# The first pair of expert blocks from counts taken before attention's last group

## The chip, the cores and the metric

The kernel runs on one core of a Trainium2 chip. Its metric is the device time of one execution in microseconds (us); the median of several executions is given, and one more execution was recorded by the hardware profiler. The names of the engines in what follows are those of the profile: PE is TensorE's matmul, PEld its weight load (which overlaps PE), DVE is VectorE, ACT is ScalarE, POOL is GpSimd, SP is SyncE, which here only issues DMAs. Each engine works through its own instructions in order; DMAs are issued from the queues of SP, ACT and POOL.

## The reference: what is computed

Three layers in a row, with B = 4, 8 heads, 768 positions, head width 48, so 3,072 tokens of width 384:

```python
for t in range(S):                        # attention, a delta rule per (batch, head)
    y[:, :, t] = einsum('bhd,bhde->bhe', q[:, :, t], state)
    v_old = einsum('bhde,bhd->bhe', state, k_n[:, :, t])
    state = state + bt * einsum('bhd,bhe->bhde', k_n[:, :, t], v[:, :, t] - v_old)
...
h = x @ w_in                              # first layer: 384 -> 2048 -> 384
x = np.maximum(0.01 * h, h) @ w_out
...
do_compute = x @ w_skip > 0               # expert layer, top 1 of 8
e_idx = argmax(x @ w_gate)                # gate_w is its softmax probability
y = gate_w * (np.maximum(x @ w1[e], 0) @ w2[e])     # w1: 384 x 1024, w2: 1024 x 384
out = x + y                               # for tokens with do_compute, else x
```

## The kernel before

**Stages.** Attention works in twelve groups of 256 tokens (a chunk of 128 positions of two batches). The first layer (`moe1`) takes each group of 256 rows when its attention is done: eight slices s of 256 hidden columns, `m_up` (matmuls into `ph`, L796) and, two slices later, `m_down` (L818 to L820, into `o`). All matmuls are split into high and low halves in fp16, so each product is three matmuls. Between them ACT copies `gg` out of PSUM (L801), DVE makes the leaky ReLU (L802), ACT casts the high half `ghh` (L804), and POOL makes the low half `gll` (L806). The twelfth group is done by `moe1_last`: it brings the ten columns with the scores first, so that the last route can start early.

**Route.** After each group `route` finds each token's expert and its place in that expert's part of the list `lst`, and POOL scatters the token numbers there, two scatters per group (L782); the second waits for the first. `store` writes the group's rows to `x2s` and to `out`, from SP's queue (from POOL's for the last group). "Route 10" is that of the eleventh group; the last route is route 11.

**Expert blocks.** A `Block` is 256, 128 ("small") or 64 ("tiny") rows of one expert. Its `tokens` loads its piece of the list (`ix`, L1189), gathers the rows from `x2s` (`xg`, L1192, one gather per 128 rows), and PE transposes them (L1200, into `pt`), from which ACT and DVE make `xh` and `xl`. Then come four `up` (L1215) and four `down` (L1233 to L1235), and `fin` scatters the result to `out` (L1246). Both the list loads and the gathers stand in POOL's queue. A gather reads `x2s`, so it waits for every store to it that was issued ahead of it. Weights of an expert are eight `ws` tiles of 384 KB, loaded from SP's queue (L1165, L1168), five in flight, and split by ACT (high, L460) and DVE (low, L461). Two successive "early" blocks belong to the same expert and share one set of weights.

**Tables.** Which expert and which rows a block has is known only at run time. `counts` takes the number of tokens per expert after a route (a matmul, L1041); `early` makes from it, after route 10, a table of up to six full blocks (pairs, from experts with at least 512 tokens so far); `tables` makes the other kinds' after the last route. SP and POOL read entries of a table with value loads (L1155). The order of blocks is fixed: four early, tiny, small, two early, then big ones (up to 256 rows, from what is left) with tiny and small ones between.

**Order.** `emit` interleaves the threads (attention's groups, `moe1`, `weights`, `tokens`, `moe2`) by a clock of PE's work; so it decides on each engine what stands ahead of what. `weights` holds the second expert's split until the last tables are placed (L1277).

Of the kernel before, what the change touches and what calls it, by code (L numbers as in the profile page):

```python
# [11 lines left out]
ALU = mybir.AluOpType  # L12
# [12 lines left out]
NE, F2 = 8, 1024  # L25
# [5 lines left out]
LR = 3072  # L31
BIG = 1 << 20
LOOK = 2
NEB, NSB, NSS, NTS = 6, 3, 3, 3
NBB = 20
NL = NE * LR + (NBB + 1) * 256
LOOK2 = 2
NET = 3, 3
NV = 8


# [471 lines left out]
def tile_kernel(ctx, tc, kq, ktok, vtok, bet, w_in, w_out, w_skip, w_gate, w1, w2, out):  # L513
    nc = tc.nc
    pool = lambda c, name, bufs, **k: c.enter_context(tc.tile_pool(name=name, bufs=bufs, **k))
# [213 lines left out]
    acc_state, routed, placed = [None], [-1], []  # L729
# [228 lines left out]
    n = len(groups)  # L958
# [14 lines left out]
    threads = [t for l in (tb, tv) for x in l for t in x.ts] + tz + tq + ta + tl + tn + tp + [Thread(loader()), tm]  # L973
# [11 lines left out]
    late = dict(side="right", reuse_waits="tile")  # L985
# [6 lines left out]
    e2 = pool(ctx, "e2", 2, **late)  # L992
    et = [pool(ctx, "et", 1, **late)]
    e3 = pool(ctx, "e3", LOOK2 + 2, **late)
    lctx = ctx.enter_context(ExitStack())
    m8 = pool(lctx, "m8", NS1 - LOOK - 2, **late)

    def moe1_last():
        i = n - 1
        scores = lambda s: m_down(i, s, slice(HD, XW), "r", ops2)  # L1000
        for s in range(NS1):
            yield from m_up(i, s, m8 if s < NS1 - LOOK - 2 else m3, h2)
            if s >= LOOK:
                yield from scores(s - LOOK)
        yield from m_down(i, 0, slice(0, HD), i)
        for s in range(NS1 - LOOK, NS1):
            yield from scores(s)
        sc = rp.tile([128, 2, 10], F32, tag="sc", name="sc")
        for t in range(2):
            nc.scalar.activation(out=sc[:, t], in_=ms["r"][t][:, HD:XW], func=AF.Copy, scale=2.0 ** -14)  # L1010
        threads.insert(0, Thread(high(last_route(i, sc), 150), lambda: "early" in state))
        for s in range(1, NS1):
            yield from m_down(i, s, slice(0, HD), i)
        xs = m_out(i, i, slice(0, HD))
        nc.vector.tensor_copy(out=xs[:, :, HD:HD + 1], in_=sc[:, :, 0:1])
        store(xs, first(i), nc.gpsimd)
        lctx.close()
        et.append(pool(ctx, "eu", 1, **late))

    def last_route(i, sc):  # L1020
        yield 0, 2
# [4 lines left out]
    t1 = lambda nm, shape, dt=F32: tbp.tile([1] + shape, dt, tag=nm, name=nm)  # L1026
# [7 lines left out]
    tt = lambda o, a, b, op: nc.vector.tensor_tensor(out=o, in0=a, in1=b, op=op)  # L1034
# [4 lines left out]
    def counts(nm):  # L1039
        pr = hps.tile([128, 512], F32, tag="h", name="cnt")  # L1040
        nc.tensor.matmul(pr[:, 0:NE], lhsT=ones16, rhs=acc_state[0], start=True, stop=True)  # L1041
        cnt = t1("cnt" + nm, [NE])
        nc.vector.tensor_copy(out=cnt, in_=pr[0:1, 0:NE])
        return cnt

    def above(x, first, nm, step=256.0):

        thr, gt, nb = t1("thr", [12]), t1("o", [NE, 12]), t1("nb" + nm, [NE])
        nc.vector.tensor_scalar(out=thr, in0=kio[:, 0:12], scalar1=step, scalar2=float(first), op0=ALU.mult, op1=ALU.add)
        tt(gt, col(x, 12), row(thr, NE), ALU.is_gt)  # L1050
        nc.vector.tensor_reduce(out=nb, in_=gt, axis=AX.X, op=ALU.add)
        return nb

    def upto(nb, nm):

        m, cb = t1("f", [NE, NE]), t1("cb" + nm, [NE])
        tt(m, tri8, row(nb, NE), ALU.mult)
        nc.vector.tensor_reduce(out=cb, in_=m, axis=AX.X, op=ALU.add)
        return cb

    def table(nb, cb, at, n, nm, step=True):
# [21 lines left out]
        state[nm] = tb  # L1083
        return last.ins

    def early():

        nb = above(counts("e"), 511.5, "e", 512.0)
        nc.vector.tensor_scalar(out=nb, in0=nb, scalar1=2.0, scalar2=None, op0=ALU.mult)
        cb = upto(nb, "e")  # L1090
        a, b, zero, taken = (t1(x, [NE]) for x in ("mine", "mina", "zero", "taken"))
        nc.vector.memset(zero, 0.0)
        table(nb, cb, zero, NEB, "early")
        tt(a, cb, nb, ALU.subtract)
        nc.vector.tensor_scalar_min(out=a, in0=a, scalar1=float(NEB))
        nc.vector.tensor_scalar_min(out=b, in0=cb, scalar1=float(NEB))
        tt(taken, b, a, ALU.subtract)
        state["taken"] = taken
        yield 0, 12
        for b in blocks[:3]:  # L1100
            yield from b.tokens()

    def tables():

# [28 lines left out]
    state = {}  # L1133

    class Block:


        def __init__(self, kind, k, ops):
            self.kind, self.k, self.ops = kind, k, ops

            self.of = blocks[-1] if kind == "early" and k % 2 else self
            self.loaded = self.split_ = 0
            self.ws, self.g = [None] * 8, {}
            self.tok = False
            self.nt = 1 if kind in ("small", "tiny") else 2
            self.rows = 64 if kind == "tiny" else 128
            self.slot = sum(b.nt == self.nt for b in blocks) % NET[self.nt - 1]
            blocks.append(self)
# [97 lines left out]
                nc.gpsimd.indirect_dma_start(out=out[:, :], out_offset=bass.IndirectOffsetOnAxis(ap=ix[:, t:t + 1], axis=0),  # L1246
                                             in_=y, in_offset=None, bounds_check=NT - 1, oob_is_err=False)

    order = [("early", 0), ("early", 1), ("early", 2), ("early", 3), ("tiny", 0), ("small", 0), ("early", 4), ("early", 5)]
    for k in range(NSB):  # L1250
        order += [("big", k)] + [(x, k + 1) for x in ("tiny", "small") if k < NSB - 1]
    blocks = []
# [4 lines left out]
    def weights():  # L1257
        own = [b for b in blocks if b.of is b]

        def more():  # L1260
            while sum(x.loaded - x.split_ for x in own) < 5:
                nxt = next((x for x in own if x.loaded < 8), None)
                if nxt is None or nxt.kind not in state:
                    break
                nxt.load()

        more()
        yield 0, 8
        for i, b in enumerate(own):
            if i > 2:  # L1270

                last = max(j for j, x in enumerate(blocks) if x.of is own[i - 3])
                yield 0, 0, lambda: ended[0] > last
            for _ in range(8):
                if b.loaded == b.split_:
                    yield 0, 0, lambda: more() or b.loaded > b.split_
                if i == 1 and not placed:  # L1277
                    yield 0, 0, lambda: placed
                with tc.issue_after(placed[0]) if i else nullcontext():
                    b.split()  # L1280
                more()
                yield 0, 0.7

    def tokens():
        for i, b in enumerate(blocks):
            if i < 3:
                continue
            same = [j for j in range(i) if blocks[j].nt == b.nt]
            yield 0, 0, lambda: b.kind in state and sum(j >= ended[0] for j in same) < NET[b.nt - 1]
            yield from b.tokens()  # L1290
# [22 lines left out]
        while pend:  # L1313
            yield from down()

    threads = [t for t in threads if not t.done] + [Thread(weights())]
    emit(threads, lambda: tm.done and routed[0] == n - 2)
    te = Thread(early())
    tl1 = Thread(moe1_last())
    threads = [te] + threads + [tl1]  # L1320
# [64 lines left out]
```

## Time and profile before

| | before |
|---|---|
| median of 3 runs | 1105.67 us (1105.28 to 1114.81) |
| the profiled execution | 1103.89 us |
| its span, first to last instruction | 1102.3 us |
| mean granted TensorE clock | 0.932 of 2.4 GHz |
| PE busy | 880.9 us, 80% of the span |
| PEld, DVE, ACT, POOL busy | 673.8, 699.7, 635.7, 517.7 us |
| DMA moved | 133.01 MB |

The profile's times are us from the start of the span. A row of the timeline gives the start, the duration, the engine, the line of the kernel, the operation with its output and inputs, the shape, how many such instructions in a row, and in brackets the time in which the engine was idle just before, with what ended that. Matmuls are pipelined, so the durations of neighbours overlap; the distance of their starts is what one costs.

### The profile page before, as it was taken

The numbers are of one execution on the slowest core, as the hardware profiler recorded it, in microseconds if no ns is written. First come the engines' busy times: TensorE is split into PE (matmuls) and PEld (weight loads), VectorE is DVE, ScalarE is ACT, GpSimd is POOL, SyncE is SP. The second block draws the span as 40 slices with busy tenths as digits, with TensorE's granted clock in tenths as the row PEclk, the third lists the DMA queues.
The fourth block names the chain that finished last, engine by engine and source line by source line (L and its number), as shares of the span: only waits on it lengthen the run. The fifth ranks groups of instructions, "written<-read, shape, count | busy, mean of one in ns | idle before, by whom it ended". The sixth has DMA issues, their size and how long they took to land. (4 is left out here: it accounts for less than half of the span.)

```text
span 1102.3 us, 26057 instructions
## 1 busy us (share of the span) xinstructions
PE 880.9 (80%) x10212; PEld 673.8 (61%) x10212; DVE 699.7 (63%) x1444; ACT 635.7 (58%) x1458; POOL 517.7 (47%) x536
## 2 busy tenths in 40 slices
PE   2167987578888778879878889899987689999893
PEld 1155765456666666657666567677765467676672
DVE  6889988758746878756657266332226575757850
ACT  4486587566867876748576657463333344545630
POOL 3567566473457566637464445352233252432110
PEclk9999987789999898989989899999999879999997
DMA  8844876662434455453412322200005376766820
GB/s 208 226 117 116 234 231 160 102 139 42 152 62 98 139 133 150 127 86 106 99 53 48 31 60 30 70 20 16 30 23 141 96 251 199 240 204 213 282 84 13
DMA packets 164880, 133.01 MB, mean 121 GB/s; under 512 B 87870, under 2 KB 146964, under 8 KB 164746
## 3 DMA queue, kind: packets, MB, share of 16 engines
q1 hardware_dynamic: 151696, 111.42, 38.4%
q10 hardware_dynamic: 8570, 10.76, 3.6%
q0 software_dynamic: 4480, 9.07, 2.7%
q8 instruction: 82, 1.34, 0.6%
q14 instruction: 52, 0.43, 0.2%
HBM read 101.68 MB, written 30.13 MB: 120 GB/s over the span
## 5 line engine op out<-in xcount | busy, mean ns | idle before, releaser
L806 POOL TENSOR_TENSOR gll<-gg,ghh 128x512 f16<-128x512 f32 x96 | 116.9, 1220 | 131.6 <-ACT ghh L804 117.0
L820 PE MATMUL o<-woh,gll 128*128 128x394 f16 (+2 forms) x416 | 128.1, 335 | 19.5 <-POOL gll L806 19.4
L796 PEld LDWEIGHTS <-wih 128*128 128x128 f16 x1152 | 115.7, 103 | 45.5 <-issue 22.5
L819 PE MATMUL o<-wol,ghh 128*128 128x394 f16 (+2 forms) x416 | 136.8, 334 | 0.0
L818 PE MATMUL o<-woh,ghh 128*128 128x394 f16 (+2 forms) x416 | 134.5, 333 | 1.0 <-ACT woh L640 0.9
L802 DVE SCALAR_TENSOR_TENSOR gg<-gg 128x512 f32<-128x512 f32 x96 | 78.5, 819 | 84.0 <-ACT gg L801 80.6
L263 POOL TENSOR_TENSOR gl<-g,gh 128x512 f16<-128x512 f32 x88 | 109.7, 1250 | 38.0 <-ACT gh L262 34.2
L254 ACT ACTIVATE g<-g,d 128x128 f32<-128x128 f32 x384 | 112.2, 389 | 18.6 <-PE g L251 10.5
L796 PE MATMUL ph<-xh,wih 128*128 128x256 f16 x576 | 103.5, 289 | 17.6 <-ACT gg L801 9.4
L796 PE MATMUL ph<-xl,wih 128*128 128x256 f16 x576 | 103.2, 287 | 1.1 <-DVE xl L726 1.1
L796 PE MATMUL ph<-xh,wil 128*128 128x256 f16 x576 | 102.6, 285 | 0.0
L255 POOL TENSOR_SCALAR_AFFINE_SELECT g<-g 128x512 f32<-128x512 f32 x96 | 71.1, 743 | 66.6 <-ACT g L254 65.9
L801 ACT COPY gg<-ph 128x512 f32<-128x512 f32 x96 | 57.4, 599 | 64.3 <-PE ph L796 60.8
L804 ACT CAST ghh<-gg 128x512 f16<-128x512 f32 x96 | 60.4, 630 | 46.8 <-DVE gg L802 46.5
L262 ACT CAST gh<-g 128x512 f16<-128x512 f32 x88 | 55.6, 636 | 41.1 <-POOL g L255 40.0
L1246 POOL DMA_INDIRECT out_dram<-y,ix x24 | 28.9, 1204 | 101.7 <-DVE y L1244 88.6
L782 POOL DMA_INDIRECT lst<-ids_i,pi x24 | 28.3, 1178 | 88.9 <-DMA lst<-ids_i,pi 53.3
L1215 PEld LDWEIGHTS <-w1h 128*128 128x128 f16 x720 | 58.5, 99 | 18.5 <-issue 8.8
L820 PEld LDWEIGHTS <-gll 128*128 128x128 f16 x416 | 40.1, 101 | 46.4 <-POOL gll L806 23.9
L1233 PE MATMUL o<-w2h,gh 128*128 128x384 f16 (+1 forms) x192 | 63.9, 333 | 1.0 <-ACT gh L1219 0.9
L796 PEld LDWEIGHTS <-wil 128*128 128x128 f16 x576 | 58.4, 103 | 10.1 <-issue 0.4
L1234 PE MATMUL o<-w2l,gh 128*128 128x384 f16 (+1 forms) x192 | 63.5, 331 | 0.0
(279 smaller groups left out, 2584.5 us busy)
## 6 DMA issues: line engine op xcount, KB each, us to landing
ws<-in_moe_w_dram SPq DMA_DIRECT2D x96, 384.0 KB, 5.2
kt<-in_ktok_dram SPq DMA_DIRECT2D x24, 384.0 KB, 3.9
x<-in_kq_dram SPq DMA_DIRECT2D x22, 384.0 KB, 4.3
sc<-hl SPq DMA_DIRECT2D x22, 384.0 KB, 3.0
raw<-in_moe_w_out_dram ACTq DMA_DIRECT2D x16, 384.0 KB, 4.7
ai<-gh SPq DMA_DIRECT2D x24, 256.0 KB, 2.8
vs<-in_vtok_dram SPq DMA_DIRECT2D x24, 192.0 KB, 3.5
x2s<-xs SPq DMA_DIRECT2D x22, 192.5 KB, 2.9
```

What stands on the lines that cost most here:

```text
L254: nc.scalar.activation(out=g32[:, j], in_=g[:, j], func=AF.Copy, scale=k["dd"][:, x, h:h + 1])
L255: nc.gpsimd.affine_select(out=g32, in_=g32, pattern=[[0, 4], [1, C]], compare_op=ALU.is_gt, fill=0.0, base=0, channel_multiplier=-1)
L263: nc.gpsimd.tensor_tensor(out=gl[:, hs], in0=g32, in1=gh[:, hs], op=ALU.subtract)
L796: nc.tensor.matmul(ph[:, j], lhsT=wt[:, d, fs], rhs=xx[:, d], start=(n == 0), stop=(n == 3 * KD - 1))
L802: nc.vector.scalar_tensor_tensor(out=g, in0=g, scalar=0.01, in1=g, op0=ALU.mult, op1=ALU.max)
L804: nc.scalar.copy(out=gh, in_=g)
L806: nc.gpsimd.tensor_tensor(out=gl, in0=g, in1=gh, op=ALU.subtract)
L818: nc.tensor.matmul(o, lhsT=gh[:, j, ts], rhs=wo[0][:, f, cols], start=(f == 0), stop=False)
L819: nc.tensor.matmul(o, lhsT=gh[:, j, ts], rhs=wo[1][:, f, cols], start=False, stop=False)
L820: nc.tensor.matmul(o, lhsT=gl[:, j, ts], rhs=wo[0][:, f, cols], start=False, stop=(f == NF1 - 1))
L1233: nc.tensor.matmul(o, lhsT=gh[:, j, ts], rhs=wh[:, f], start=(f == 0), stop=False)
L1234: nc.tensor.matmul(o, lhsT=gh[:, j, ts], rhs=wl[:, f], start=False, stop=False)
```

## The change

A new kind of block, "first", takes the first two places of the order (`NFB` = 2); the early ones go from six to four. A new thread, `beforehand`, starts as soon as `routed[0]` is n − 4, which is to say when only the routes of the last three groups are outstanding. It takes the counts of that moment, makes the table of the "first" pair by the rules that `early` had (now in `pairs`), lists and gathers both blocks' rows at once, and transposes them as the other threads leave room. `weights` starts loading with that table, among the last groups of the first layer. `early` then makes its table from the counts after route 10, less the blocks already taken. The second expert's split no longer waits for the last tables, only the third's does. The pool `eu` opens earlier, and the one-tile kinds ("tiny", "small") have two sets of buffers in place of three. With the reference's inputs the order of blocks still begins with two of one expert and two of another.

```diff
-NEB, NSB, NSS, NTS = 6, 3, 3, 3
+NFB, NEB, NSB, NSS, NTS = 2, 4, 3, 3, 3
...
-NET = 3, 3
+NET = 2, 3
...
+    et.append(pool(ctx, "eu", 1, **late))
...
-        et.append(pool(ctx, "eu", 1, **late))
...
+    def pairs(nm, had, n):
+
+        nb = above(counts(nm), 511.5, nm, 512.0)
+        at, a, b, taken = (t1(x + nm, [NE]) for x in ("at", "mine", "mina", "taken"))
+        nc.vector.tensor_scalar(out=at, in0=had, scalar1=256.0, scalar2=None, op0=ALU.mult)
+        stt(nb, nb, 2.0, had, ALU.mult, ALU.subtract)
+        cb = upto(nb, nm)
+        table(nb, cb, at, n, nm)
+        tt(a, cb, nb, ALU.subtract)
+        nc.vector.tensor_scalar_min(out=a, in0=a, scalar1=float(n))
+        nc.vector.tensor_scalar_min(out=b, in0=cb, scalar1=float(n))
+        tt(taken, b, a, ALU.subtract)
+        tt(taken, taken, had, ALU.add)
+        state["taken"] = taken
+
+    def beforehand():
+
+        zero = t1("zero", [NE])
+        nc.vector.memset(zero, 0.0)
+        pairs("first", zero, NFB)
+        gens = [b.tokens() for b in blocks[:NFB]]
+        for g in gens:
+            next(g)
+        yield 0, 12
+        for g in gens:
+            yield from g
+
     def early():
...
+        pairs("early", state["taken"], NEB)
+        g = blocks[NFB].tokens()
+        next(g)
         yield 0, 12
-        for b in blocks[:3]:
-            yield from b.tokens()
+        yield from g
...
-            self.of = blocks[-1] if kind == "early" and k % 2 else self
+            self.of = blocks[-1] if kind in ("first", "early") and k % 2 else self
...
-    order = [("early", 0), ("early", 1), ("early", 2), ("early", 3), ("tiny", 0), ("small", 0), ("early", 4), ("early", 5)]
+    order = [("first", 0), ("first", 1), ("early", 0), ("early", 1), ("tiny", 0), ("small", 0), ("early", 2), ("early", 3)]
...
-                if i == 1 and not placed:
+                if i == 2 and not placed:
                     yield 0, 0, lambda: placed
-                with tc.issue_after(placed[0]) if i else nullcontext():
+                with tc.issue_after(placed[0]) if i > 1 else nullcontext():
                     b.split()
...
     def tokens():
         for i, b in enumerate(blocks):
-            if i < 3:
+            if i <= NFB:
                 continue
...
-    threads = [t for t in threads if not t.done] + [Thread(weights())]
+    threads = [t for t in threads if not t.done] + [Thread(weights()), Thread(beforehand(), lambda: routed[0] >= n - 4)]
```

The rows below are the instructions as each engine has them in its program, first those of before, then those of the changed kernel. The first place is POOL's, around the two list scatters of route 10 (`lst<-ids_i,pi`; those of route 9 stand some rows ahead). Before, block 0's list (`ix<-lst`) comes behind both:

```order
L782 DMA lst<-ids_i,pi 29952x1
L806 TENSOR_TENSOR gll<-gg,ghh 128x512
L782 DMA lst<-ids_i,pi 29952x1
L806 TENSOR_TENSOR gll<-gg,ghh 128x512 x2
L1155 TENSOR_LOAD tbearly
L1155 ISA x2
L1189 REGISTER_ALU
L1189 DMA ix<-lst 128x2
L1155 TENSOR_LOAD tbearly
L1155 ISA x2
L806 TENSOR_TENSOR gll<-gg,ghh 128x512
```

In the changed kernel the piece begins with block 1's list load (block 0's stands just ahead of it) and ends with block 2's:

```order
L1207 DMA ix<-lst 128x2
L806 TENSOR_TENSOR gll<-gg,ghh 128x512
L1210 DMA xg<-x2s,ix 128x385 x4
L782 DMA lst<-ids_i,pi 29952x1
L806 TENSOR_TENSOR gll<-gg,ghh 128x512 x2
L782 DMA lst<-ids_i,pi 29952x1
L806 TENSOR_TENSOR gll<-gg,ghh 128x512 x2
L1173 TENSOR_LOAD tbearly
L1173 ISA x2
L1207 REGISTER_ALU
L1207 DMA ix<-lst 128x2
```

The four gathers of the first pair, and all that they wait for, stand ahead of route 10's scatters and of the last four `gll` of the first layer. SP's queue has, in the changed kernel, these rows where the weights start; before, the two `x2s` stores (of the eleventh group) stood right behind the two `out_dram` ones, and the value load and all `ws` behind them:

```order
L735 DMA out_dram<-xs 128x384 x2
L1173 TENSOR_LOAD tbfirst
L1173 ISA x2
L1183 ISA
L1183 DMA ws<-in_moe_w_dram 128x3x256
L1183 ISA
L1183 DMA ws<-in_moe_w_dram 128x3x256
L1183 ISA
L1183 DMA ws<-in_moe_w_dram 128x3x256
L733 DMA x2s<-xs 128x385 x2
```

Three loads of weights have moved ahead of the two stores for which the gathers wait. The second place is ACT's, from the `gg` copy of the last group's fourth slice on. Before, all eight copies are done ahead of the first weight split:

```order
L801 COPY gg<-ph 128x512
L804 CAST ghh<-gg 128x512
L801 COPY gg<-ph 128x512
L804 CAST ghh<-gg 128x512
L460 ACTIVATE w1h<-ws 128x3x256 x4
L1010 ACTIVATE sc<-o 128x10 x2
```

In the changed kernel the eight splits of the first expert's weights (`w1h`, `w2h`) stand among the copies of the fifth to the eighth slice:

```order
L801 COPY gg<-ph 128x512
L804 CAST ghh<-gg 128x512
L460 ACTIVATE w1h<-ws 128x3x256
L801 COPY gg<-ph 128x512
L460 ACTIVATE w1h<-ws 128x3x256 x2
L804 CAST ghh<-gg 128x512
L801 COPY gg<-ph 128x512
L460 ACTIVATE w1h<-ws 128x3x256
L460 ACTIVATE w2h<-ws 128x768
L804 CAST ghh<-gg 128x512
L460 ACTIVATE w2h<-ws 128x768 x3
L801 COPY gg<-ph 128x512 x2
```

The copy of the fifth slice is now behind one split, those of the last two behind all eight. The third place is PE's. Block 0's and block 1's transposes stand, but for the last, among the last group's `m_down` in the changed kernel. Between block 0's second up and its first down there are these rows, in which `pt<-ident,xg` is block 2's first three transposes:

```order
L1233 MATMUL ph<-xh,w1l 128x256
L1041 LDWEIGHTS ones_166
L1041 MATMUL cnt<-acc,ones_166 128x8
L1218 MATMUL pt<-ident,xg 128x128 x3
L1251 LDWEIGHTS gh
L1251 MATMUL o<-w2h,gh 128x384
L1252 LDWEIGHTS gh
```

So PE can't go on with block 0's first down until it has block 2's first rows. Before, the transposes that stood there were none; block 1's came within block 0's fourth up:

```order
L1215 MATMUL ph<-xh,w1l 128x256
L1215 LDWEIGHTS w1h
L1215 MATMUL ph<-xh,w1h 128x256
L1200 MATMUL pt<-ident,xg 128x128 x3
L1215 LDWEIGHTS w1h
```

## Rows read from the trace of the kernel before

**Rows 1.** Busy time by stretch: length, PE, PEld, DVE, ACT, POOL, clock, DMA share, GB/s
```profile
838.00:863.00 25.00, 18.78 (x121) 10.58 (x119) 11.67 (x37) 13.41 (x21) 4.88 (x5) 0.86 0.79 220
863.00:905.00 42.00, 30.43 (x195) 21.82 (x195) 26.26 (x82) 11.87 (x18) 18.09 (x19) 0.80 0.48 150
905.00:1085.00 180.00, 171.84 (x1529) 125.33 (x1526) 115.50 (x171) 89.01 (x148) 48.74 (x46) 1.00 0.61 195
```
**Rows 2.** PE's waits from 836 to 905: total us, times, longest
```profile
PE pt L1200 <- DMA xg<-x2s,ix: 14.3, 3, 8.5
```
**Rows 3.** PE's timeline, from 815 to 905
```profile
817.95 0.49 PE L796 MATMUL ph<-xh,wih 128*128 128x256 f16 x3
...
854.80 0.55 PE L1200 MATMUL pt<-ident,xg 128*128 128x128 f32 x3 [2.77 <-DMA xg<-x2s,ix]
...
863.01 0.82 PE L1215 MATMUL ph<-xh,w1h 128*128 128x256 f16 x6 [1.36 <-ACT xh L1202]
...
866.94 0.33 PE L1233 MATMUL o<-w2h,gh 128*128 128x384 f16 x1
867.10 0.33 PE L1234 MATMUL o<-w2l,gh 128*128 128x384 f16 x1
...
881.30 0.90 PE L1200 MATMUL pt<-ident,xg 128*128 128x128 f32 x3 [8.54 <-DMA xg<-x2s,ix]
...
897.84 0.88 PE L1200 MATMUL pt<-ident,xg 128*128 128x128 f32 x3 [3.02 <-DMA xg<-x2s,ix]
```
**Rows 4.** PE by stretch: length, busy, granted clock, DMA share, GB/s
```profile
856.00:859.40 3.40, 3.40 (x17) 0.50 0.98 321
881.30:886.70 5.40, 5.40 (x21) 0.50 0.28 100
897.80:903.80 6.00, 5.96 (x26) 0.50 1.04 322
```
**Rows 5.** POOL's timeline, from 825 to 905
```profile
829.25 0.99 POOL L782 DMA_INDIRECT lst<-ids_i,pi  x1 [1.19 <-PE cnt L1041]
...
834.46 0.99 POOL L782 DMA_INDIRECT lst<-ids_i,pi  x1 [3.03 <-DMA lst<-ids_i,pi]
835.48 2.27 POOL L806 TENSOR_TENSOR gll<-gg,ghh 128x512 f16<-128x512 f32 x2
842.37 0.61 POOL L1189 DMA_DIRECT2D ix<-lst  x1 [4.62 <-DMA lst<-ids_i,pi]
...
849.49 1.10 POOL L1192 DMA_INDIRECT xg<-x2s,ix  x1 [5.27 <-DMA ix<-lst]
850.90 1.00 POOL L1192 DMA_INDIRECT xg<-x2s,ix  x1 [0.31 <-issue]
...
875.20 1.73 POOL L1189 DMA_DIRECT2D ix<-lst  x3 [7.26 <-DMA lst<-ids_i,pi]
...
887.45 4.18 POOL L1192 DMA_INDIRECT xg<-x2s,ix  x1 [3.25 <-DVE w1l L461]
```
**Rows 6.** DVE's timeline: the early table's first and last row, one long row, weight splits
```profile
829.11 0.15 DVE L1043 COPY cnte<-cnt 1x8 f32<-1x8 f32 x1
...
834.99 2.79 DVE L1065 TENSOR_SCALAR of<-kio 1x8 f32<-1x8 f32 x1
...
837.96 0.16 DVE L1082 TENSOR_SCALAR tbearly<-sm 1x6 int32<-1x6 f32 x1
...
886.26 3.55 DVE L461 SCALAR_TENSOR_TENSOR w1l<-ws,w1h 128x768 f16<-128x768 f32 x4
```
**Rows 7.** SP's timeline: the first issues of weights
```profile
835.96 2.23 SPq L1165 DMA_DIRECT2D ws<-in_moe_w_dram  x4
```
**Rows 8.** ACT's timeline: the first and the last split of block 0's weights
```profile
845.56 0.84 ACT L460 ACTIVATE w1h<-ws 128x768 f16<-128x768 f32 x1 [6.20 <-DMA ws<-in_moe_w_dram]
...
854.26 0.84 ACT L460 ACTIVATE w2h<-ws 128x768 f16<-128x768 f32 x1 [0.16 <-DMA ws<-in_moe_w_dram]
```
**Rows 9.** The page's DMA issues: count, KB each, median us from issue to landing
```profile
ws<-in_moe_w_dram SPq DMA_DIRECT2D x96, 384.0 KB, 5.2
```

More of the change, by code (lines that the diff above doesn't have):

```diff
@@ L1084, in table @@
         return last.ins
-    def early():
[L1088 to L1098, printed above, removed]
+    def pairs(nm, had, n):
[21 more added lines that the diff above has]
+            yield from g
+    def early():
+        pairs("early", state["taken"], NEB)
+        g = blocks[NFB].tokens()
+        next(g)
         yield 0, 12
-        for b in blocks[:3]:
-            yield from b.tokens()
+        yield from g
     def tables():
```

## The prediction

> **What bounds the kernel now.** I read the busy table first, then the work by stretches, then PE's waits there, then the engines that it waits for. From 905 us on PE is busy 171.84 of 180.00 us at full clock [rows 1], so the end moves with whatever PE loses ahead of 905. Two stretches are thin: 838 to 863, 18.78 us of 25.00 busy, and 863 to 905, 30.43 of 42.00 [rows 1]. In both, PE waits for gathered rows: 14.3 us in three waits [rows 2]. The rows of PE's timeline show them at 854.80 (2.77), 881.30 (8.54) and 897.84 (3.02), with a 1.36 wait for ScalarE's cast at 863.01, where block 0's first matmul starts [rows 3]. After the three gaps the granted clock stands at 0.50 to 0.51, which is the lower of its two levels: 3.4 us from 856.0, 5.4 us from 881.3, 6.0 us from 897.8 [rows 4]. Half of such a stretch is lost.
>
> So from block 0's first matmul (863.01) on, PE loses 8.54 + 3.02 of waiting and (5.4 + 6.0)/2 = 5.7 of clock: **17.3 us**. That is all that earlier blocks can win there. Ahead of 863.01 it also loses 2.77 + 1.36 and 1.7 of clock to the same cause.
>
> Why the rows are late is read from POOL [rows 5]. The first `lst` scatter of route 10 goes at 829.25, the second at 834.46, because it waits 3.03 for the first. The list load of block 0 goes at 842.37, the gathers at 849.49 and 850.90, and PE has the rows at 854.80: 25.5 us from the first scatter. Block 1's list load stands at 875.20, behind the last route's scatters (7.26 idle for them).
>
> **What the change moves, and the costs.** Nothing is computed twice: the counts of the reference's inputs give one expert 1,111 tokens after ten groups, so both "first" blocks are full, and the number of blocks stays. PE gets one counting matmul, DVE 39 operations on one partition, and the one-tile blocks (tiny and small) keep two of their three slots. The lost slot I cost at nothing: what covers it is the block of 256 rows that stands between two pairs of one-tile blocks in the order, about as long as the 12.4 us that a list load and its gather take (842.37 to 854.80 [rows 5, 3]); were that cover gone, each of three such blocks could wait a part of 12.4.
>
> *Table.* The count goes where PE stands at 817.95 [rows 3]. In the kernel before, the early table takes DVE from 829.11 to 838.12 [rows 6], 9.0 us; the first table has a few rows more. One of its rows takes 2.79 instead of 0.15, beside two `gll` of POOL at 835.48 that take 2.27 [rows 5, 6]; the same `gll` stand beside the new table, so I repeat 9.0: ready at 827.2 (2 us earlier if no row is held), and SP's first `ws` at 827.7.
>
> *Rows.* On SP group 10's `x2s` stores now stand behind three `ws`. Four issues took 2.23 [rows 7], so the stores go at 829.6. What they then take is not shown: the first `ws` of before came 9.6 us after its issue (835.96 to ScalarE's split at 845.56 [rows 7, 8]), all `ws` on the median 5.2 [rows 9]. I take the 9.6, since they go into the queue right behind those first loads: 839.2, 840 for the second; the gathers start at 840.6. The lower end is 835.1, set by the list load (842.37 until its gather at 849.49 is 7.1, from about 828).
>
> *POOL.* Four gathers at 1.4 each (849.49 to 850.90) hold POOL until 846.2. Behind them in order: the first scatter of route 10, two `gll`, the second scatter 5.2 later, two `gll`. These scatters went at 829.25 and 834.46 before, so they lose 17 us. That is the price of the change: the last group's four `gll` end at 846.2 + 5.2 + 1.0 + 2.3 = 854.7. Behind the last of them PE has, by the order, 59 matmuls, 50 of them at 0.163 (the rows 866.94 and 867.10 [rows 3]) and the rest tiny: 8.4. **Block 0 starts at 863.1**, as before, although it waits for nothing of its own any more. ScalarE could spoil this: by the order its copy of the last group's fifth `gg` stands behind the first weight split, and the last two copies behind all eight, since ScalarE works in order. The eight take 9.5 us (845.56 to 855.10 [rows 8]). From 827.7 + 9.6 = 837.3, with the copies between them, that is 848, and the last `gll` could go at 851; POOL comes to it at about 853.5. So PE's last ups wait some 6 us for their buffer, but under the wait for `gll`; the cover is 2 us thick, and what goes beyond it shifts block 0. Route 10 also starts some 3 us later on DVE; its scatters wait for the gathers anyway.
>
> *Block 2.* Its list needs route 10's second scatter. I take the chain of before, 25.5 from the first scatter: 846.2 + 25.5 = 871.7. PE's order puts its first transposes behind block 0's first two ups. Two ups are 863.01 to 866.94, 3.93 [rows 3], with the transposes and the last route's few matmuls between them 4.6. PE gets there at 867.7 and waits 4.0. From 871.7 it goes on as if block 0 had started at 867.1. Against 863.0 that is a loss of 4.1, plus 1.7 of clock (3.4 us at half, as after the gap of 2.77). Block 3's rows need the last route's scatters and block 0's slot; they come in POOL's order before PE's place for them at about 895 to 900, at no cost, 2 us if late. The second expert's weights are issued behind the first's and used only after blocks 0 and 1, some 30 us of PE later.
>
> **Sum:** 17.3 − 4.1 − 1.7 = 11.5 us less than the profiled execution's own 1103.89: 1092.4. The median of the runs is 1105.67, 1.8 above that execution, so 1094.2; I say **1094**. About 1% (11 us) is what a measurement of this kernel can tell from no change: faster is below 1094.6, slower above 1116.7.
>
> One rule speaks against the change. The row: in one case a gather's issue took 4.18 on POOL, at 887.45, while DVE ran four weight splits without a break from 886.26 (3.55) [rows 5, 6]; those at 849.49 and 850.90 took 1.10 and 1.00, beside single splits. The Trainium skill, page "SBUF — State Buffer", section "🔬 SBUF: two separate sides", says that VectorE and GpSimd share a port pair as a lock held for a whole instruction, and that GpSimd cannot write its DMAs' descriptors while VectorE holds it. The 4.18 row and the 2.79 row agree with it, the 1.00 row doesn't ask for it. By that rule all six gathers that now stand beside splits would take 4.18, as priced under the third rival.
>
> **Rivals.**
> 1. *Fast start* (1088.5): the first loads don't lag, the gathers go at 835.1. Route 10's scatters, the `gll` and block 2's rows all come 5.5 earlier; block 0 starts at 857.6, the wait for block 2 stays 4.0. The gain is 11.5 + 5.5 = 17.0: 1086.9, or 1088.5 on the median. For it: the 5.2 of all `ws` [rows 9]. Against it: the 9.6 of the first [rows 7, 8].
> 2. *The wait moves* (1101): block 2's gather is as slow as that of 887.45, which PE waited for until 897.84, 10.4 instead of the 5.3 of 849.49 to 854.80 [rows 5, 3], some 6 us more with its longer issue, because block 1's weights load beside it. PE waits 10 instead of 4, and loses 1.3 more of clock: 1092.4 + 7.3 = 1099.7, 1101.5 on the median.
> 3. *Gathers held by splits* (1114): DVE now splits block 0's weights where the four gathers issue, and block 1's where block 2's two do. At 4.18 each instead of 1.02, six give 19.0 on POOL, all ahead of block 2's rows: 890.7. As if block 0 had started at 886.1, with 3 us of clock: 23.1 + 3.0 − 17.3 = 8.8 slower, 1112.7, 1114.5 on the median. It decides from four such gathers on (12.6 us, above the 11.5 gained); block 3's two would add 6.3 more. For it: the 4.18 row. Against it: the two gathers of 1.10 and 1.00, and that a split waits for a `ws` of its own, which breaks the run of splits.
> 4. *No effect* (1105.7): block 0 and 1 wait as before. The order speaks against it.
>
> **How the numbers follow.** Forecast 0.42 (1090 to 1098), fast start 0.25, moved wait 0.22, held gathers 0.08, none 0.03. Faster by over 1%: the fast start and about half of the forecast, 0.47. Slower by over 1%: the worse part of the third rival, 0.05. Within: 0.48. The range 1086 to 1107 holds the forecast, the moved wait, no effect and most of the fast start, 0.84.
>
> **What would show it.** Block 0's first up within 2 us of 863, with no wait for its transposes; no wait for block 1's rows at all; one wait of about 4 us for block 2's, right behind two ups; the first `lst` scatter of route 10 at about 846; ScalarE idle up to 837 for the first `ws`. The forecast is wrong if the gathers issue near 835 or after 843, if any of them takes 4 us, or if PE waits for something else ahead of 905: the counts' rows on DVE, or the first expert's weights. After 905 PE should be as busy as now.

## The result and the profile after

The changed kernel's median is 1082.41 us (1077.43 to 1092.28, 4 runs); the kernel before, 1105.47 with the run taken beside it (1097.59 to 1114.81, 4 runs). The comparison of the runs gives a ratio of 0.987, 95% interval 0.9827 to 0.9912: 1.3% faster, within 0.9 and 1.7%. On 1105.5 that is 1091, where 1094 was forecast. The ratio is not the quotient of the two medians: these lie further apart, by 23 us, and 1082.41 itself stands below the forecast's range of 1086 to 1107. The run named `again` below, beside many more of before on one chip, gives 1090.41 against 1102.46, ratio 0.9892 (0.9846 to 0.9938).

The profiled execution of after took 1081.11 us. How much of the distance to 1103.89 belongs to the change is read from one place that both programs have, the last one up to which PE's program is the same. In the changed kernel the first count stands there, at 808.93; the kernel before has no such count, and reaches the same place at 817.95 [rows 3]. So 9.0 us of the distance lie in front of the change. The twelve other profiles have that place between 810.0 and 822.4 us (the table below): the front differs from run to run. From this place ("the count" in what follows) to PE's last matmul it took 265.5 us before (to 1083.43) and 251.5 after (to 1060.47), 14.0 less. This stretch, "the changed part", is what the experiments compare.

Where in it: PE's waits after, from 815 to 905 (total us, times, longest), against the 14.3 us for gathers of [rows 2]:

```profile
PE pt L1218 <- DVE xl L1221: 4.9, 2, 2.7
PE o L820 <- POOL gll L806: 3.5, 2, 2.8
PE o L818 <- ACT ghh L804: 1.8, 1, 1.8
PE pt L1218 <- DMA xg<-x2s,ix: 1.1, 1, 1.1
```

The waits for gathered rows have gone but for 1.1 us. In their place PE waits twice for `xl`, DVE's low half of the rows just transposed, which must leave PSUM before the next transposes go in. PE's timeline after, around block 0's start (start, duration, idle before in brackets), answers to [rows 3]:

```profile
850.04 0.55 PE L1218 MATMUL pt<-ident,xg 128*128 128x128 f32 x3 [2.28 <-DVE xl L1221]
...
853.84 0.49 PE L1233 MATMUL ph<-xh,w1h 128*128 128x256 f16 x3
...
857.98 0.55 PE L1218 MATMUL pt<-ident,xg 128*128 128x128 f32 x3 [2.66 <-DVE xl L1221]
...
860.24 0.84 PE L1233 MATMUL ph<-xl,w1h 128*128 128x256 f16 x3
...
863.03 0.53 PE L1218 MATMUL pt<-ident,xg 128*128 128x128 f32 x3
863.40 0.33 PE L1251 MATMUL o<-w2h,gh 128*128 128x384 f16 x1
```

Block 0's first matmul stands 44.9 us after the count (853.84 − 808.93; before 45.1), its first down at 54.5 (before 866.94 − 817.95 = 49.0). A triple of `ph` takes 0.64 instead of 0.33 behind the second of the two waits: the granted clock is 0.50 to 0.53, about its lower level, from 859.0 to 862.5. Block 2's transposes at 863.03 wait for nothing. POOL's timeline after, the answer to [rows 5]:

```profile
828.05 1.09 POOL L1210 DMA_INDIRECT xg<-x2s,ix  x1 [6.44 <-DMA ws<-in_moe_w_dram]
829.44 1.04 POOL L1210 DMA_INDIRECT xg<-x2s,ix  x1 [0.30 <-issue]
830.79 1.01 POOL L1210 DMA_INDIRECT xg<-x2s,ix  x1 [0.30 <-issue]
832.10 1.75 POOL L1210 DMA_INDIRECT xg<-x2s,ix  x1 [0.30 <-issue]
834.15 1.11 POOL L782 DMA_INDIRECT lst<-ids_i,pi  x1 [0.30 <-issue]
...
839.76 1.00 POOL L782 DMA_INDIRECT lst<-ids_i,pi  x1 [2.20 <-DMA lst<-ids_i,pi]
...
847.78 0.60 POOL L1207 DMA_DIRECT2D ix<-lst  x1 [4.72 <-DMA lst<-ids_i,pi]
853.69 1.17 POOL L1210 DMA_INDIRECT xg<-x2s,ix  x1 [5.31 <-DMA ix<-lst]
```

The profile puts the 6.44 in front of the first gather down to a weight load, which a gather doesn't need; it reads `x2s`, and the two stores to it had landed by 827.06. The first pair's gathers go 19.1 us after the count, route 10's first scatter at 25.2, block 2's gathers at 44.8 and 46.2. And the work from block 0's first down to the end, before and then after (length, PE busy, granted clock, DMA share, GB/s):

```profile
866.00:1084.00 218.00, 199.28 (x1697) 0.96 0.59 190
```

```profile
863.40:1061.00 197.60, 190.77 (x1679) 1.00 0.61 196
```

That is the gain: the granted clock is 1.00 on the mean instead of 0.96, and PE's idle time falls from 18.7 us to 6.8.

### The profile page after: what moved, and what is told of

Same layout as the page of the kernel before. It is cut to its first block, busy times and chain, and to the rows that moved or that the text cites. A ratio compares the mean times of both kernels' runs of the same rounds, so it can differ in the third digit from the quotient of the medians.

```text
span 1079.5 us, 26091 instructions
## 1 busy us (share of the span) xinstructions
PE 872.8 (81%) x10213; PEld 670.1 (62%) x10213; DVE 707.7 (66%) x1474; ACT 634.6 (59%) x1458; POOL 512.3 (47%) x536
## 5 line engine op out<-in xcount | busy, mean ns | idle before, releaser
L796 PEld LDWEIGHTS <-wih 128*128 128x128 f16 x1152 | 113.5, 101 | 45.0 <-issue 24.0
L802 DVE SCALAR_TENSOR_TENSOR gg<-gg 128x512 f32<-128x512 f32 x96 | 80.8, 842 | 83.7 <-ACT gg L801 82.9
L796 PE MATMUL ph<-xh,wih 128*128 128x256 f16 x576 | 101.1, 283 | 19.7 <-ACT gg L801 11.9
L1264 POOL DMA_INDIRECT out_dram<-y,ix x24 | 25.2, 1052 | 97.5 <-DVE y L1262 85.5
L461 DVE SCALAR_TENSOR_TENSOR w1l<-ws,w1h 128x768 f16<-128x768 f32 x48 | 45.1, 955 | 32.5 <-ACT w1h L460 32.2
L782 POOL DMA_INDIRECT lst<-ids_i,pi x24 | 26.4, 1102 | 79.9 <-DMA lst<-ids_i,pi 54.6
```

Source lines behind the costliest of these rows:

```text
L796: nc.tensor.matmul(ph[:, j], lhsT=wt[:, d, fs], rhs=xx[:, d], start=(n == 0), stop=(n == 3 * KD - 1))
L802: nc.vector.scalar_tensor_tensor(out=g, in0=g, scalar=0.01, in1=g, op0=ALU.mult, op1=ALU.max)
```

## The experiments

All kernels of the table were compared with the kernel before on the same chip; the ratio is to it. The columns after it come from one profile each, in us: the place of the first count (`before` and `b_net` have none: for the one it is the place above, for the other it is worked out from the early count at 827.17, 10.92 behind it in the kernel before), and, counted from there, block 0's first up, its first down, and PE's last matmul (its start); then the time from that down to the last matmul.

| kernel | ratio (95%) | count at | first up | first down | last matmul | down to last |
|---|---|---|---|---|---|---|
| before | 1 | 817.95 | 45.1 | 49.0 | 265.5 | 216.5 |
| changed | 0.987 (0.9827, 0.9912) | 808.93 | 44.9 | 54.5 | 251.5 | 197.1 |
| again | 0.9892 (0.9846, 0.9938) | 814.85 | 48.3 | 54.6 | 258.2 | 203.6 |
| rows_late | 1.0117 (1.0035, 1.0199) | 815.04 | 51.4 | 56.4 | 274.9 | 218.5 |
| w_late | 0.9896 (0.9827, 0.9965) | 819.87 | 50.7 | 56.8 | 256.6 | 199.8 |
| one_early | 0.9941 (0.9905, 0.9976) | 810.03 | 46.4 | 52.5 | 253.9 | 201.4 |
| hold | 0.990 (0.987, 0.9931) | 819.90 | 42.6 | 50.1 | 247.8 | 197.7 |
| undo_hold | 0.9925 (0.9886, 0.9964) | 818.59 | 50.5 | 54.8 | 252.3 | 197.5 |
| x2s_first | 0.9883 (0.9807, 0.9959) | 817.69 | 43.0 | 53.8 | 250.2 | 196.5 |
| hold_x2s | 0.9877 (0.9819, 0.9936) | 821.32 | 44.3 | 55.9 | 255.9 | 200.0 |
| quiet | 0.9883 (0.9836, 0.993) | 820.73 | 41.1 | 53.6 | 255.9 | 202.3 |
| quiet_hold | 0.9879 (0.9828, 0.9929) | 822.36 | 45.7 | 51.8 | 253.2 | 201.5 |
| quiet_hold_x2s | 0.9899 (0.9852, 0.9947) | 815.52 | 48.6 | 53.1 | 255.7 | 202.6 |
| b_net | 0.9968 (0.9926, 1.0009) | 816.25 | 45.0 | 48.9 | 265.0 | 216.0 |

The last column splits the table in two: the eleven profiles in which POOL has block 1's list and gathers ahead of the last route's scatters have 196.5 to 203.6, the three in which it has them behind (`before`, `b_net`, `rows_late`) 216.0 to 218.5. The places of block 0 show no such split.

**again**: no edit.

> The changed kernel once more, beside the kernel before on the same chip. In the two profiles the first count matmul stands at 808.93 (before, the same place: 817.95) and PE's last matmul at 1060.47 (before: 1083.43). So the changed part takes 251.5 us where it took 265.5, 14.0 less; the other 9.0 us lie in attention and in the first layer, where both programs have the same PE rows. Theory: only the 14 us belong to the change; the ratio stays at 0.987 (1091 by the before of 1105.5) and the changed part at 250 to 253. Rival: the front is really faster (by the other placement of buffers): the ratio comes to 0.979 and the place of the first count lies 9 us ahead of that of the kernel before again.

The ratio came as the theory has it, the changed part longer than it said, 258.2: two profiles of one program are 6.6 us apart. They lie behind block 0's first down, where PE waits 6.0 us for gathered rows instead of 1.8, and where one stretch of 50 us (from 180 after the count) has PE busy for 44.04 instead of 46.61, at a granted clock of 0.93 instead of 1.00. So a single profile can't tell 4 us. The front was not ahead again (814.85, within the spread of the table).

**rows_late**: the rows after route 10 again, the weights early. `beforehand` makes only the table; POOL reads its entries from a copy that DVE makes behind the early table, and `early` fetches the rows of the first three blocks.

```diff
-        gens = [b.tokens() for b in blocks[:NFB]]
-        for g in gens:
-            next(g)
-        yield 0, 12
-        for g in gens:
-            yield from g
+        yield 0, 0
...
-        g = blocks[NFB].tokens()
-        next(g)
         yield 0, 12
-        yield from g
+        for b in blocks[:NFB + 1]:
+            yield from b.tokens()
```

> The changed kernel with the first pair's lists and rows fetched only after route 10 again, as before; its weights still come early. Theory (the rows are the gain): the waits for block 0's and block 1's gathers are back, the changed part takes 262 to 268 us, no faster than before. Rival (the weights' earlier loads are a good part of the gain): 255 to 259.

The whole gain is gone, and 1.2% more; the changed part, 274.9, is longer than the theory's 262 to 268. PE's waits of this kernel, and the rows on PE's timeline behind them:

```profile
PE pt L1219 <- DMA xg<-x2s,ix: 12.9, 2, 11.4
PE pt L1219 <- DVE xl L1222: 5.0, 2, 4.0
```

```profile
864.94 0.90 PE L1219 MATMUL pt<-ident,xg 128*128 128x128 f32 x3 [4.03 <-DVE xl L1222]
866.42 1.44 PE L1234 MATMUL ph<-xh,w1h 128*128 128x256 f16 x6 [0.58 <-ACT xh L1221]
883.67 0.87 PE L1219 MATMUL pt<-ident,xg 128*128 128x128 f32 x3 [11.41 <-DMA xg<-x2s,ix]
```

The long wait for block 1's rows is back, 11.4 instead of 8.54 [rows 3]. So late rows cost the gain. But these rows are later than those of before: block 0's list load goes 35.2 us after the count (850.28) instead of 24.4 (842.37 [rows 5]), and on DVE the low halves of the first expert's weights now stand among the rows of the early table, which is ready 33.6 us after the count instead of 20.2. So this kernel doesn't show what early weights are worth with rows no later than before; whether they are needed, the next one shows.

**w_late**: the rows early, the first expert's weights as late as before (SP reads the index from the same kind of copy).

```diff
-    threads = [t for t in threads if not t.done] + [Thread(weights()), Thread(beforehand(), lambda: routed[0] >= n - 4)]
+    threads = [t for t in threads if not t.done] + [Thread(weights(), lambda: "later" in state), Thread(beforehand(), lambda: routed[0] >= n - 4)]
```

> The changed kernel with the first pair's rows early as they are, but the first expert's weights loaded only after the early table is written (after route 10, as before). The count that begins the changed part stands 45 us ahead of block 0's first matmul. Theory (the rows are the gain, the weights only have to be there): the stores to x2s no longer stand behind three weight loads, so the four gathers go 3 to 4 us earlier; the weights land about 40 us after the count and hold block 0 by a few us; ratio to the kernel before 0.985 to 0.995, changed part 249 to 256. Rival (the weights beside the first layer's last groups are needed): block 0 and block 2 wait for weights, 260 or more.

The first load goes 18.5 us after the count, where the kernel before had 18.0. The gathers go at 834.72, 14.9 after the count, as the theory has it, and the ratio, 0.9896, is that of `again`; the changed part, 256.6, is just above the theory's range. Block 0 starts later (50.7), but not for its weights: PE waits 3.78 us until 870.23 for block 2's rows, whose transposes stand ahead of block 0's first up in this kernel. The weights need not be early: the rows alone bring the gain.

**one_early**: block 1's list and rows together with block 2's, after route 10: the first edit is in `beforehand`, the second in `early`.

```diff
-        gens = [b.tokens() for b in blocks[:NFB]]
+        g = blocks[0].tokens()
...
-        g = blocks[NFB].tokens()
+        gens = [b.tokens() for b in blocks[1:NFB + 1]]
```

> The changed kernel with block 0's rows early, but block 1's list and rows after route 10, with block 2's. Theory: route 10's scatters come earlier on POOL, since only two gathers or none stand ahead of them, and block 1's rows are there in time, because it starts some 16 us after block 0; what counted is that neither waits for the last route's scatters: 248 to 256 us, as the changed kernel. Rival (the early rows of block 1 are the gain, its 8.54 us wait and 2.7 of clock): 260 or more.

The changed part is 253.9, as the theory has it, and far from the rival's 260; the ratio, 0.9941, lies just above the upper ends of the changed kernel's two intervals (0.9912 and 0.9938). PE waits 6.1 us for gathers, in three waits of at most 3.1. So it is enough to lift block 1 over the last route's scatters; whether its still earlier place is worth the half per cent isn't settled, since the intervals overlap.

**hold** and **undo_hold**: when the second expert's splits run. In `hold` they are ordered behind block 1's last `xh` on ACT (`last.lh`) and its last `xl` on DVE (`last.ll`):

```diff
+                last = blocks[NFB - 1]
+                if i == 1 and not last.tok:
+                    yield 0, 0, lambda: last.tok
...
-                with tc.issue_after(placed[0]) if i > 1 else nullcontext():
-                    b.split()
+                with tc.issue_after(last.lh if i == 1 else placed[0]) if i else nullcontext():
+                    with tc.issue_after(last.ll) if i == 1 else nullcontext():
+                        b.split()
```

In `undo_hold` that part of the change is taken back:

```diff
-                if i == 2 and not placed:
+                if i == 1 and not placed:
...
-                with tc.issue_after(placed[0]) if i > 1 else nullcontext():
+                with tc.issue_after(placed[0]) if i else nullcontext():
```

> The changed kernel, with the second expert's splits ordered behind block 1's last xh on ACT and its last xl on DVE. In the changed kernel PE waits 2.28 and 2.66 for DVE's xl behind those splits, right around block 0's first ups, and the clock is at half for 3.5 us after. Theory (the splits that run too early cause this): both waits go, 5 to 6.6 us less in the changed part, 245 to 247 us. Rival (the splits are then late for block 2, whose ups come about 31 us after block 0's): PE waits for block 2's weights, the part takes 251 or more.

> The changed kernel with one part undone: the second expert's split waits for the last tables again. Theory: on DVE the low halves come after the last tables, some 20 us later, on ACT most high halves still stand ahead of xh; so one of the two waits of PE for xl stays: 248 to 251 us for the changed part. Rival (the low halves are needed earlier, the early split is a part of the gain): block 2 waits for its weights, 255 or more.

In `hold` the waits for `xl` are gone, and one of 2.7 has come, which the profile puts down to DVE's row `f` of the last tables:

```profile
PE o L818 <- ACT ghh L804: 2.8, 1, 2.8
PE pt L1218 <- DVE f L1034: 2.7, 1, 2.7
PE o L820 <- POOL gll L806: 2.3, 4, 0.7
```

On PE's timeline this wait stands behind the ups, ahead of block 2's first transposes:

```profile
866.08 0.49 PE L1233 MATMUL ph<-xl,w1h 128*128 128x256 f16 x3
869.32 0.52 PE L1218 MATMUL pt<-ident,xg 128*128 128x128 f32 x3 [2.75 <-DVE f L1034]
```

A transpose reads nothing of the tables. It reads block 2's rows, and their first gather, issued at 864.99, landed at 869.18. So this is read as the wait for block 2's rows that the prediction has; in `hold_x2s` below the same transposes wait 5.71 us, there put down to the gather itself. The first down comes 4.4 us earlier (50.1), and the part is the shortest of all, 247.8, between the theory's 245 to 247 and the rival's 251. In `undo_hold` neither wait for `xl` stays, against the theory; PE waits 4.8 for the last route's `oh` on DVE instead, and the part is 252.3, just above the forecast 248 to 251. Against the kernel before, 0.990 and 0.9925: the whole kernel doesn't show the 4 us.

**x2s_first** and **hold_x2s**: SP stores group 10's rows (the last of `stored`) ahead of the first loads of weights.

```diff
-                nxt.load()
+                with tc.issue_after(stored[2 * (n - 1) - 1]):
+                    nxt.load()
```

> The changed kernel with group 10's two stores to x2s ahead of the first weight loads on SP. In the changed kernel POOL is idle for 6.4 us until these stores have landed, 8 us after their issue, then issues the gathers at 828.05, 19.1 us after the count. Theory (the loads in front delay the stores): the gathers go 3 to 4 us earlier, at 15 to 16 us after the count, route 10's scatters and the last gll with them; PE's waits for gll and block 0's start come forward by 2 to 4 us; changed part 248 to 251. Rival (the gathers wait for something else, the list): no earlier than 19.

> The edits of hold and x2s_first together, with the first expert's splits among the last group's copies as in the changed kernel. Theory: the waits for xl go (hold: 4.5 us to block 0's first down), the gathers go earlier but one of them meets an unbroken run of splits on DVE again and takes over 4 us: 245 to 250 us, ratio 0.983 to 0.989. Rival: the fourth gather takes 1.0 to 1.8 as in the changed kernel.

The gathers of `x2s_first` go 14.9 after the count, where the changed kernel has 19.1: the loads in front did delay the stores. (Block 0's list doesn't explain the 19.1: in the changed kernel it had landed at 824.94, 2.1 us ahead of the second store.) POOL's timeline, and then DVE's beside the fourth gather:

```profile
832.61 1.08 POOL L1210 DMA_INDIRECT xg<-x2s,ix  x1 [2.25 <-DMA x2s<-xs]
...
835.33 1.00 POOL L1210 DMA_INDIRECT xg<-x2s,ix  x1 [0.30 <-issue]
836.64 4.59 POOL L1210 DMA_INDIRECT xg<-x2s,ix  x1 [0.31 <-issue]
841.53 1.04 POOL L782 DMA_INDIRECT lst<-ids_i,pi  x1 [0.30 <-DVE w2l L461]
```

```profile
837.36 0.94 DVE L461 SCALAR_TENSOR_TENSOR w1l<-ws,w1h 128x768 f16<-128x768 f32 x1
...
838.37 0.94 DVE L461 SCALAR_TENSOR_TENSOR w1l<-ws,w1h 128x768 f16<-128x768 f32 x1
...
839.42 0.94 DVE L461 SCALAR_TENSOR_TENSOR w1l<-ws,w1h 128x768 f16<-128x768 f32 x1
...
840.53 0.96 DVE L461 SCALAR_TENSOR_TENSOR w2l<-ws,w2h 128x768 f16<-128x768 f32 x1
```

The fourth gather takes 4.59 while DVE splits without a break, as the one of 887.45 in [rows 5, 6], and eats 3.6 of the 4.2 us won. In `hold_x2s` the same gather took 4.78, and block 2's first one 3.33 beside three splits, for whose rows PE then waited the 5.71. The part of `x2s_first`, 250.2, is in the expected range; that of `hold_x2s`, 255.9, is not (245 to 250). By the ratio neither kernel is told apart from the changed one.

**quiet**, **quiet_hold**, **quiet_hold_x2s**: the first expert's splits behind the last group's copies (`tail` holds ACT's and DVE's last rows of the last `m_up`), then with the other two edits.

```diff
+                if i == 0 and not tail:
+                    yield 0, 0, lambda: tail
...
+                with tc.issue_after(placed[0] if i else tail[0]) if i != 1 else nullcontext():
+                    with tc.issue_after(tail[1]) if i == 0 else nullcontext():
```

> The changed kernel with the first expert's splits ordered behind the last group's last gg and ghh on DVE and ACT; their loads still start early. In the changed kernel ACT's copy and cast of the last slices stand behind splits that wait for their loads, and PE waits 1.8 to 3.1 us for ghh; on DVE the splits run beside the four gathers, whose fourth took 1.75 and 1.83 us in two runs, and 4.59 where the splits ran without a break. Theory: PE's wait for ghh goes, all four gathers take about 1.0 us; block 0's splits then come later, and block 0 starts no earlier, since only five loads are ahead: changed part 246 to 252 us. Rival (the splits are then what block 0 waits for): 254 or more.

> The edit of quiet and that of hold together: the first expert's splits behind the last group's copies, the second's behind block 1's last xh and xl. Theory: PE's waits for ghh and for xl both go, 3 + 4.5 us and the clock around them; changed part 243 to 247, ratio to the kernel before 0.980 to 0.986. Rival (ACT and DVE then have 16 splits ahead of block 2 and the wait moves to block 0's gh or block 2's weights): 250 or more, ratio 0.988 to 0.995, no better than the changed kernel.

> As quiet_hold, and the stores to x2s ahead of the weight loads on SP. Theory: the four gathers go some 15 us after the count (19.1 in the changed kernel) at 1.0 us each, so route 10's scatters and block 2's rows come 4 to 5 us earlier; as nothing splits beside them, the gain of x2s_first is not lost to a gather of 4.59: 241 to 246 us, ratio 0.978 to 0.985, the fastest. Rival: no wait for rows is left to be won, so it equals quiet_hold.

With no split beside them all four gathers are quick, in `quiet` and here in `quiet_hold_x2s`, from 14.9 after the count on:

```profile
830.45 1.17 POOL L1212 DMA_INDIRECT xg<-x2s,ix  x1 [2.27 <-DMA x2s<-xs]
831.92 1.01 POOL L1212 DMA_INDIRECT xg<-x2s,ix  x1 [0.30 <-issue]
833.24 1.00 POOL L1212 DMA_INDIRECT xg<-x2s,ix  x1 [0.30 <-DVE tbearly L1084]
834.54 0.99 POOL L1212 DMA_INDIRECT xg<-x2s,ix  x1 [0.30 <-issue]
```

But PE then waits elsewhere, in `quiet_hold_x2s`:

```profile
PE o L822 <- POOL gll L806: 6.7, 1, 6.7
PE pt L1220 <- DMA xg<-x2s,ix: 2.9, 1, 2.9
PE o L1253 <- ACT gh L1239: 2.9, 1, 2.9
```

PE waits 6.7 for the last `gll` of POOL, which stands there behind block 2's list load (849.18, idle for 5.80 before it, for route 10's second scatter), then for ACT, which now has the late splits ahead of block 0's `gh`. In `quiet` PE waits 4.0 for block 0's own rows and 4.0 for `xl`, behind splits that had waited for their loads; in `quiet_hold` 4.0 for block 0's rows and 3.7 for `oh`. The expected 0.980 to 0.986 and 0.978 to 0.985 did not come: 0.9879 and 0.9899, and 0.9883 for `quiet`, whose part is 255.9, which is its rival's value. The parts of the other two, 253.2 and 255.7, missed their ranges as well. In these kernels shortening one of the waits ahead of block 0's downs gave the next one, and none can be told from the changed kernel.

**b_net**: `NET = 2, 3` alone, in the kernel before.

> The kernel before with one edit of the change alone: two sets of buffers for the tiny and small blocks in place of three. Theory (the lost slot is covered by the blocks of 256 rows between): 1.000, within 0.4%. Rival (the slots are awaited): up to 12 us more, 1.005 to 1.011.

0.9968, the interval holds 1; the changed part and block 0's places are those of the kernel before. There the third slot was not awaited.

## Why the prediction was right, step by step

- **The 17.3 us that go.** From block 0's first down on, the profile of before has 216.5 us, the changed kernel 197.1 and 203.6 in two profiles, 19.4 and 12.9 less: 16.2 on the mean. `w_late` (199.8, the rows early and the weights not) and `rows_late` (218.5, the weights early and the rows not) show that it is the rows. Right, as closely as two profiles that differ by 6.5 can tell.
- **Block 0 starts where it did.** Forecast 45.1 after the count, measured 44.9 and 48.3. The 44.9 is in part luck. POOL's last `gll` ended at 843.05, 34.1 after the count instead of 36.8, and a wait for `xl` that the forecast did not have (2.28 at 850.04) took most of these 2.6 us back. Without this wait block 0 would have started at 42.6, as it does in `hold`. The terms on the way were off too: the table took 7.9 instead of 9.0 (DVE 809.17 to 817.07; four one-partition rows there took 0.84 to 1.14 beside POOL's `gll`), the gathers went at 19.1 instead of 22.7, route 10's first scatter at 25.2 instead of 28.3.
- **The first loads lag 9.6 us.** Wrong: the first `ws` was issued at 817.58 and split at 820.87, 3.3 later. From the first `x2s` store behind the loads to the first gather it took 8.7, 819.34 to 828.05, where the forecast had 11.0 (829.6 to 840.6); `x2s_first` shows that the loads in front delay the stores: 5.3 there (827.28 to 832.61).
- **5.8 us lost between the first ups and downs** (a wait of 4.0 for block 2's rows, 0.1 of start, 1.7 of clock). In the first profile the sum came out, 54.5 − 44.9 − 3.9 = 5.7, by luck; in `again` it is 54.6 − 48.3 − 3.9 = 2.4. The wait of the forecast did not show in the changed kernel. Block 2's rows were there: the scatter that they hang on came 3 us earlier than forecast, and 2.28 and 2.66 us of another wait stood ahead of them. What I had not costed is an edge of the change: the second expert's splits, no longer held, stand ahead of `xh` and `xl` on ACT and DVE, and the first of them waited for its own load:

```profile
847.69 0.84 ACT L460 ACTIVATE w1h<-ws 128x768 f16<-128x768 f32 x1 [8.09 <-DMA ws<-in_moe_w_dram]
848.44 0.47 ACT L1220 ACTIVATE xh<-pt 128x384 f16<-128x384 f32 x1
```

  The transposes at 842.38 were done, but `xh` came at 848.44, `xl` at 849.44, and PE waited 2.28 at 850.04. `hold` takes these waits away and has the first down 4.4 earlier, and there the forecast's own wait appears, 2.75 us for block 2's rows (5.71 in `hold_x2s`). So the forecast had a wait that is real, and missed the one that stands in front of it.
- **ScalarE's splits among the last copies** were costed at nothing, with 2 us of cover. They make PE wait 1.8 for `ghh` (826.33; 3.1 in `again`), and behind that it still waits 3.5 (1.6) for POOL's `gll`. So in the changed kernel the cover was there. `quiet` removes the wait for `ghh`, and PE waits for rows and `xl` instead.
- **The weights and the slots at nothing.** Right for the first expert's weights (`w_late`) and, as far as the kernel before shows it, for the slots (`b_net`). For the second expert's weights it was wrong: their splits are what stands ahead of `xl`.
- **The rivals.** The held gathers are real, 4.59 and 4.78 in two of the experiments; in the changed kernel the worst of the six that the rival counts took 1.75 (1.83 in `again`). The fast start came in part: its gathers stand 17.2 after the count, those of the forecast 22.7, the measured ones 19.1 and 19.7. The moved wait did not come as told, since block 2's gathers took 1.17 and 1.01 and PE did not wait for them. No effect is excluded by the ratio.
- **What would show it.** Of the signs named, the one wait for block 2's rows and ScalarE idle up to 837 (19 after the count; its first split came 11.9 after) did not show. And PE does wait for something else ahead of 905, for `xl`; such a wait the prediction names as a sign of being wrong. So the gain and its size were forecast for the right reason, the price for a reason that was only half of it.

What stays open: which of the variants is best by a few tenths of a per cent. The intervals are 0.3 to 0.8% wide to either side, and one program's changed part differs by 6.6 us between two profiles. Nor do the runs show why the front of the first profile was 9 us short.

## What to carry to other kernels

A serial chain of small DMAs (scatter, list, gather) is worth lifting over the next such chain as a whole: what paid was to have two blocks' rows before the last route's scatters got into the queue. The gain can be read from the timeline as the sum of the waits and of the lower clock behind them; what is moved in front lengthens other chains, so look for what stands behind each moved instruction on every engine, the in-order neighbours of a load that may be late above all. And when one of several waits of like size is removed ahead of a join, expect the next one to take its place. Where the profile names what ended a wait, ask whether the waiting instruction reads anything of it: the 2.75 of `hold` and the 6.44 of the changed kernel were put down to rows that were not the cause.

## What the hardware showed that was not expected

- A gather's issue on POOL took 0.98 to 1.24 us in the 107 cases of all fourteen traces in which DVE ran no split beside it, even amid a run of DVE's one-partition rows of 0.15 to 0.2. Beside splits, of about 0.95 each, it took 0.95 to 1.84 in 222 cases, and 2.86 to 4.78 in seven, all beside three or four splits with at most short rows between. The rule of the Trainium skill, page "SBUF — State Buffer", section "🔬 SBUF: two separate sides" (a shared port pair, locked for a whole instruction), agrees with the long ones. But a run of splits without a pause is not enough: in the kernel before the gather at 950.01 took 1.03 beside splits that follow each other from 949.14 on. What decides isn't shown.
- The first load of an expert's weights was split 9.6 us after its issue in the kernel before [rows 7, 8]; in the changed one it was 3.3 for the first expert and 7.4 for the second (840.33 to 847.69). No run here shows why.
